# Last output tile written instead of accumulated, and list scatters without a memset behind their pacing copy

## The chip, the cores and the metric

The kernel runs on one core of a Trainium2 chip. The metric is the device time of one execution in microseconds (us). TensorE (PE) does the matmuls, VectorE (DVE) and ScalarE (ACT) empty the accumulators, GpSimd (POOL) issues the indirect DMAs and does some elementwise work, SyncE (SP) issues the plain DMAs.

## The reference

A linear attention with decay (4 batches, 8 heads, 768 positions, blocks of 64) gives 3072 tokens of 512 numbers. Behind it stands a mixture of 8 experts: each token goes to the two experts with the highest noisy logits, with two softmax weights, and its output row is the sum of the two experts' rows. Cut to what matters here:

```python
noisy_logits = x @ w_gate + log1p(exp(x @ w_noise)) * noise
top2 = argpartition(-noisy_logits, 2, axis=1)[:, :2]      # top2_w: softmax of the two
out = zeros((3072, 512))
for e in range(8):
    for k in range(2):
        mask = top2[:, k] == e
        h = maximum(x[mask] @ w1[e], 0.0)
        out[mask] += top2_w[mask, k, None] * (h @ w2[e])
```

Everything is float32; the kernel splits each factor of a matmul into a high and a low part and sums three products.

## The kernel before

The attention runs first, over twelve units of two chunks. While it runs, the routing works out, for each token and each of its two choices, a row of a list in DRAM (`lst`, one stretch per expert). 48 indirect DMAs on POOL (`scatter_list`, line 631) write 128 list entries each. They are not issued in one go: `routing` puts them into `scatters`, and `paced(n, tile)` (line 680) issues up to n of them at a chosen place of the program. `paced` first copies one element of a tile into a 1x1 `spacer` on POOL, so that POOL waits there until that tile has been made, and then calls `scatter(n)`, which calls `scatter_list` for each. `scatter_list` begins with a memset of the same `spacer` (line 633), then the indirect DMA (line 634). Some scatters are issued without `paced`, by `scatter` alone (from `finish` and in the main line).

Expert 0 is worked on with indices found directly. From expert 1 on an expert's list is read from DRAM (`load_rec`), its token rows are gathered (`gather_rows`, line 889, indirect DMAs on POOL), turned, split and multiplied by w1 (experts 2 to 7 by a scheme with seven products, `first_layer`), and then by w2 in tiles of 128 tokens (`gemm2`, line 1067). The experts 1 to 7 are ordered by load. Expert 7 of that order has six tiles, worked on in the order 0, 3, 1, 4, 2, 5; a list's unused places hold an index that is out of bounds, and the DMA skips it.

A tile of `gemm2` ends so: VectorE multiplies the accumulated rows by the tokens' weights (`tensor_scalar`, line 1094) into a staging tile, and `scatter_out` (line 1133) does a memset of `spacer` on POOL and an indirect DMA that writes the 128 rows to `out` (line 1135). For expert 0 it writes plainly; for the others it carries `compute_op` ADD, so that the DMA adds to what `out` holds. The scatters of one expert don't wait for one another; the first tile of an expert waits for those of the expert before. `out` is filled with zeros during the attention.

After the first layer of expert 7 POOL gets a `drain` (line 1474). Behind the last tile stands a loop for tokens beyond an expert's capacity (`For_i`, line 1520), with no iteration for these inputs. The tile `zero` (128 rows of 512) is used as a staging buffer when rows are turned, last for expert 7.

Of the kernel before, what the change touches and what calls it, by code (L numbers as in the profile page):

```python
# [37 lines left out]
E = 8  # L38
F = 1024
FB = F // 128  # L40
NTOK = B * S
# [44 lines left out]
def tiles(e):  # L86

    return NT if TAILS[e] else NT - 1


def size(e, t):
    return TS if t < NT - 1 else TAILS[e]
# [31 lines left out]
def kernel(  # L124
# [3 lines left out]
    nc = tc.nc  # L128
    MULT, ADD, SUB = OP.mult, OP.add, OP.subtract
# [62 lines left out]
    for i in range(7):  # L192
        n = 1 << i
# [3 lines left out]
    p = psum.tile([128, H], FT, name="pL")  # L197
# [13 lines left out]
    p = psum.tile([128, HP, C], FT, name="pL")  # L211
# [69 lines left out]
    jobs, scatters, PL = [], [], {}  # L281
# [15 lines left out]
        if all_scattered:  # L297
            scatter(len(scatters))

    def scatter(n):  # L300
        for job in scatters[:n]:
            scatter_list(*job)
        del scatters[:n]

    qT, qTs, kT, KD, AT, XO, XP, PO, SA, first = {}, {}, {}, {}, {}, {}, {}, {}, {}, {}
# [322 lines left out]
    lst_st, lst_ld = [], []  # L628
    spacer = consts.tile([1, 1], FT, name="spacer")

    def scatter_list(b, c, i):
        r = RT[b]
        nc.gpsimd.memset(spacer, 0.0)
        st = nc.gpsimd.indirect_dma_start(  # L634
            out=lst, out_offset=bass.IndirectOffsetOnAxis(ap=r["dest"][:, i, c:c + 1], axis=0),
            in_=r["rec"][:, c, i, :], in_offset=None)
        for s in lst_st:
            tc.declare_no_dep(st.ins, s.ins, reason="every pair of token and choice has its own row")
        for g, s in lst_ld:
            if g < b:  # L640
                tc.declare_no_dep(st.ins, s.ins, reason="a later group writes no row of an earlier group's part")
        lst_st.append(st)
# [37 lines left out]
    def paced(n, tile):  # L680
        if scatters:
            nc.gpsimd.tensor_copy(spacer, tile[0:1, 0:1])
            scatter(n)


    WB = wp.tile([128, (2 * DB - 1) * F], FR, name="w1")
# [6 lines left out]
    for n in range(2):  # L693
        o, m = n * DB * CAP, DB * TX * TS
# [11 lines left out]
    WS, REC, PV, HT, XB, WX = {}, {}, [], [], [], []  # L706
# [141 lines left out]
    def parts(e):  # L848
        if not e:
            return [(sum(PARTS0[:i]), n) for i, n in enumerate(PARTS0)]  # L850
        return [(0, PARTS1[0]), (PARTS1[0], PARTS1[1])]

    def tile_order(e):

        if e < 2:
            return [t0 + t for t0, n in parts(e) for t in range(n)]
        return [0, 3, 1, 4, 2, 5, 6][:tiles(e)]
# [198 lines left out]

    ahead = []
    OT = []

    def ring():  # L1060
        OT.append(OT.pop(0))
        return OT[-1]

# [3 lines left out]
    def gemm2(e, t):  # L1067
        n = size(e, t)
        p = psum.tile([128, DM], FT, name=next(bank2))
        if n == TS:  # L1070
            for i, (f, a, b) in enumerate(TERMS):
                if e < 2:
                    h = ht(e, a, f, slice(t * TS, t * TS + n))
                else:
                    h = hv(e, a, f, t // 3)[:, t % 3 * TS:(t % 3 + 1) * TS]
                if i == KEPT:
                    yield
                nc.tensor.matmul(p, h, W2[b][f // 2][:, f % 2, :], start=(i == 0), stop=(i == len(TERMS) - 1))  # L1078
        else:
            yield  # L1080
            for i in range(2 * FB):
                f, b = i // 2, i % 2
                nc.tensor.matmul(p[:2 * n, :], HT[0].rearrange("p (f c) -> p f c", f=FB)[:, f, FULL:FULL + 2 * n],
                                 W2[b][f // 2][:, f % 2, :], start=(i == 0), stop=(i == 2 * FB - 1))
        o = ahead.pop() if ahead else ring() if e else PV[t]
        w = REC[e, t][:, 1:2].bitcast(FT)
        if n < TS:
            o = o[:n, :]
            nc.scalar.activation(o, p[n:2 * n, :], AF.Copy)
            nc.vector.tensor_add(o, o, p[:n, :])  # L1090
            p = o
        if e in CROSS and n == TS:
            o, p = o.rearrange("p (b d c) -> p b d c", b=DB, c=32), p.rearrange("p (d b c) -> p b d c", b=DB, c=32)
        nc.vector.tensor_scalar(o, p, w, None, op0=MULT)  # L1094
        if e:
            scatter_out(e, t, o if n < TS or e not in CROSS else o.rearrange("p b d c -> p (b d c)"))

# [35 lines left out]
    def scatter_out(e, t, o):  # L1133
        nc.gpsimd.memset(spacer, 0.0)
        st = nc.gpsimd.indirect_dma_start(  # L1135
            out=out, out_offset=bass.IndirectOffsetOnAxis(ap=REC[e, t][:, 0:1], axis=0), in_=o, in_offset=None,
            bounds_check=NTOK - 1, oob_is_err=False, **({"compute_op": ADD} if e else {}))
        if t == 0:
            out_st.clear()
        for s in out_st:  # L1140
            tc.declare_no_dep(st.ins, s.ins, reason="an expert has a token once")
        out_st.append(st)

    zero = consts.tile([128, DM], FT, name="zero")
# [10 lines left out]
    for t in range(NST):  # L1155
# [19 lines left out]
        if u == NST:  # L1175
            scatter(1)
# [47 lines left out]
    XR.append(hp.tile([128, DM], FT, name="xr2"))  # L1224
    OT.extend(hp.tile([128, DM], FT, name=f"ot{i}") for i in range(5))
    PV.append(ring())
# [220 lines left out]
    for e in range(1, E):  # L1447
        if e == E - 1:
            n_over = nc.values_load(ntot[0:1, 0:1], min_val=0, max_val=MAXOV)
        if e == 1:  # L1450
            prepare(2)
            for i, (t0, n) in enumerate(parts(e)):
                for f in range(FB):
                    gemm1(e, t0, n, f)
                    if f >= 4:
                        next(ovj, None)
                    if i and f >= LAG:
                        turn_next(f - LAG)
                    if i == 0 and f % 2 == 0:
                        split_w(2, e, f // 2)  # L1460
                    if i and f < 2:
                        load_c(2, f)
                    if f < tiles(e):
                        nc.gpsimd.tensor_copy(spacer, ht(e, 0, f, columns(e, t0, n))[0:1, 0:1].bitcast(FT))
                        if t0 == 0:
                            scatter_out(0, f, PV[f][:size(0, f), :])
                        else:
                            gather_rows(2, tile_order(2)[f])
        else:
            if e == 2:  # L1470
                OT.insert(0, GT)
            step, todo = first_layer(e)
        if e == E - 1:
            nc.gpsimd.drain()
        if e == 1:
            WX.append(wp.tile([128, F], FT, name="w1b"))
            XB.append(hp.tile([128, 6 * 2 * HW], FR, name="xb"))
        if e in CROSS:
            cr = [ring() if j < NT - 1 else hp.tile([128, 128], FT, name="crt")
                  for j in CT]  # L1480
            steps = [columns2(e, d, cr) for d in range(DB)] + [gemm2(e, t) for t in (0, 1, 3, 4)]
        else:
            steps = [gemm2(e, t) for t in (tile_order(e) if e > 1 else range(NT))]
        if e > 1:
            next(steps[0])
            for i, (f, m) in enumerate(ENDS):
                step(len(SEQ) + i, f, m)
            for s in sorted(todo):
                for op in todo[s]:
                    op()  # L1490
            next(steps[1])
        if e + 1 < E:
            fetch_pairs(e + 1)
            if e > 1:
                fetch_rest(e + 1)
        if e + 2 < E and e not in CROSS:
            prepare(e + 2)
        for t, tile in enumerate(steps):
            if e == 1:
                turn_next(t + FB - LAG)  # L1500
            if e in CROSS and t == DB:
                ahead.append(ring())
                cx = [fetch_crossed(e, j) for j in CT]
                load_c(e + 1, 2)
                prepare(e + 2)
            behind(e, t)
            if e in CROSS and t > DB:
                for i in {DB + 1: (0, 1), DB + 2: (2,)}.get(t, ()):
                    add_crossed(e, CT[i], cx[i])
            last(tile)  # L1510
            if e in CROSS:
                if t == DB - 1:
                    for i, c in enumerate(cr):
                        nc.sync.dma_start(crossed[i], c)
            if e == 1:
                next(ovj, None)
                if t == 1:
                    fetch_rest(2)
    W1[1][DB - 1] = wp.tile([128, F], FR, name="w1b")
    with tc.For_i(0, n_over) as it:  # L1520
# [9 lines left out]
                                     bounds_check=NTOK - 1, oob_is_err=False)  # L1530
# [6 lines left out]
        for f in range(FB):  # L1537
            p = psum.tile([128, OV], FT, name="pS", bufs=4)
# [7 lines left out]
        p = psum.tile([OV, DM], FT, name="pO")  # L1546
        for f in range(FB):
            for i, (a, b) in enumerate(((0, 0), (0, 1), (1, 0))):
                nc.tensor.matmul(p, ht(0, a, f, slice(0, OV)), W2[b][f // 2][:, f % 2, :],
                                 start=(f == 0 and i == 0), stop=(f == FB - 1 and i == 2))  # L1550
        o = ring()[:OV]
        nc.vector.scalar_tensor_tensor(o, p, r[:, 1:2].bitcast(FT), zero, op0=MULT, op1=ADD)
        nc.gpsimd.indirect_dma_start(out=out, out_offset=off, in_=o, in_offset=None,
                                     bounds_check=NTOK - 1, oob_is_err=False)
# [27 lines left out]
```

## Time and profile before

| | us |
|---|---|
| median of 3 runs | 696.99 (695.52 to 699.48) |
| profiled execution | 693.23 |
| span of the profiled execution | 691.4 |

| engine | busy us | share of the span |
|---|---|---|
| PE | 671.6 | 97% |
| DVE | 482.4 | 70% |
| POOL | 370.0 | 54% |
| ACT | 309.5 | 45% |

The span runs from the first to the last recorded event of the profiled execution. "Idle before" is the time in which an engine had nothing running ahead of an instruction, with what ended it. Times "to landing" run from the start of a DMA's issuing instruction to the end of the transfer. A DMA issued by POOL has a row of its own on POOL (DMA_INDIRECT).

### The profile page before, as it was taken

The page shows a single profiled execution, that of the slowest core. Times are in us where ns is not written, and L with a number is a line of the kernel's source. Part 1 is how long each engine was busy: PE and PEld are TensorE (multiplying, and loading weights), DVE is VectorE, ACT ScalarE, POOL GpSimd, SP SyncE. Part 2 cuts the span into 40 slices and gives each one's busy share as a digit, 9 for nine tenths or more (in the row PEclk, how much of TensorE's full clock was granted, in tenths as well). Part 3 has the DMA queues.
Part 4 walks back from the last instruction along what each step waited for, and adds up shares of the span by engine and source line. Part 5 has one row for each costly group of instructions (what it writes and reads, how often), then busy time and mean ns, then how long its engine had stood idle before and what let it go on. Part 6 is the DMA issues. An engine that isn't in the chain of part 4 may idle for free.

```text
span 691.4 us, 13961 instructions
## 1 busy us (share of the span) xinstructions
PE 671.6 (97%) x4861; PEld 598.1 (87%) x4861; DVE 482.4 (70%) x1060; ACT 309.5 (45%) x634; POOL 370.0 (54%) x474
## 2 busy tenths in 40 slices
PE   7899999899999999999999999999999999999995
PEld 4788888698898898899989998998898899889984
DVE  6335888878436566789867886889596979588610
ACT  2667786441133332365437434653363356327400
POOL 7111355678854555776358536753773667264332
PEclk9999999999999999999999999999999999999998
DMA  9999999576517437766477547854875576464033
GB/s 205 214 233 262 229 252 250 163 245 163 113 32 221 136 119 171 175 177 191 149 183 188 189 149 178 221 175 142 166 235 158 126 195 189 122 135 116 1 46 40
DMA packets 151901, 115.06 MB, mean 166 GB/s; under 512 B 88063, under 2 KB 123007, under 8 KB 151828
## 3 DMA queue, kind: packets, MB, share of 16 engines
q1 hardware_dynamic: 137636, 84.04, 44.8%
q0 software_dynamic: 13776, 29.57, 20.5%
q8 instruction: 39, 0.64, 0.4%
q10 hardware_dynamic: 416, 0.53, 0.3%
q14 instruction: 34, 0.28, 0.1%
HBM read 77.58 MB, written 37.32 MB: 166 GB/s over the span
## 4 chain that ended last, share of the span: by engine, by line
PE 68%; DVE 12%; issue 8%; POOL 4%; DMA 3%; SPq 2%; ACT 1%; POOLq 1%; DVEq 0%
PE pS L993 15%; PE pKV L1078 13%; PE pO L1078 10%; PE pS L1037 7%; PE pS L1110 5%; PE pS L364 3%; PE pKV L377 2%; POOL lst L634 2%; PE pO L377 2%; SPq L160 2%; PE pR L993 1%; POOL out_dram L1135 1%; DMA xr<-x_tok,rec 1%; DVE ht L1004 1%; PE pS L437 1%
## 5 line engine op out<-in xcount | busy, mean ns | idle before, releaser
L993 PE MATMUL pS<-xa,w 128*128 128x400 f32 (+1 forms) x624 | 158.0, 343 | 0.3 <-ACT gt L1012 0.2
L818 POOL TENSOR_TENSOR wst<-wst 128x256 f32<-128x256 f32 x96 | 96.4, 1016 | 84.1 <-DVE w L810 81.7
L993 PEld LDWEIGHTS pS<-xa,w 128*128 128x128 f32 x624 | 113.2, 188 | 4.6 <-DVE w L810 2.0
L1135 POOL DMA_INDIRECT out_dram<-ot,rec x40 | 73.6, 1839 | 75.5 <-DVE ot L1094 56.2
L1078 PE MATMUL pKV<-w2h,ht 128*128 128x512 f32 x336 | 109.0, 394 | 0.0
L1078 PE MATMUL pO<-w2h,ht 128*128 128x512 f32 x336 | 108.4, 392 | 0.0
L993 PE MATMUL pS<-xb,w 128*128 128x400 f32 (+1 forms) x240 | 81.6, 340 | 0.0
L1078 PEld LDWEIGHTS pKV<-w2h,ht 128*128 128x128 f32 x336 | 63.2, 188 | 14.3 <-DVE gt L1094 0.6
L1078 PEld LDWEIGHTS pO<-w2h,ht 128*128 128x128 f32 x336 | 63.1, 188 | 13.5
L1037 PE MATMUL pS<-xa,w 128*128 128x256 f32 (+2 forms) x440 | 73.5, 316 | 0.8 <-DVE xa L901 0.4
L1037 PEld LDWEIGHTS pS<-xa,w 128*128 128x128 f32 x440 | 65.3, 189 | 4.9 <-DVE xa L901 0.6
L1078 PE MATMUL pKV<-w2l,ht 128*128 128x512 f32 x168 | 65.8, 391 | 0.0
L1078 PE MATMUL pO<-w2l,ht 128*128 128x512 f32 x168 | 65.7, 391 | 0.0
L961 ACT ACTIVATE xa<-wst 128x512 fp32r<-128x512 f32 (+1 forms) x48 | 25.1, 568 | 79.5 <-DVE wst L970 72.3
L810 DVE TENSOR_TENSOR w<-wst,w 128x512 fp32r<-128x512 f32 (+2 forms) x72 | 59.6, 844 | 0.1
L889 POOL DMA_INDIRECT xr<-x_tok,rec x42 | 46.2, 1101 | 19.2 <-issue 6.5
L634 POOL DMA_INDIRECT lst<-recs,dest x48 | 49.7, 1035 | 10.8 <-issue 8.5
L1012 ACT ACTIVATE ot<-pS 128x400 f32<-128x400 f32 (+1 forms) x60 | 29.7, 495 | 48.8 <-PE pS L993 44.6
L808 ACT ACTIVATE w<-wst 128x512 fp32r<-128x512 f32 (+2 forms) x72 | 48.1, 692 | 5.3 <-POOL wst L818 5.2
L1004 DVE SCALAR_TENSOR_TENSOR ht<-ot,ht 128x400 fp32r<-128x400 f32 (+1 forms) x60 | 45.4, 756 | 1.5 <-ACT ht L1001 0.8
L993 PEld LDWEIGHTS pS<-xb,w 128*128 128x128 f32 x240 | 45.0, 188 | 0.6 <-DVE xb L962 0.3
L1043 ACT ACTIVATE ht<-pS 128x256 fp32r<-128x256 f32 (+2 forms) x40 | 17.9, 448 | 59.5 <-PE pS L1037 58.2
(287 smaller groups left out, 1367.0 us busy)
## 6 DMA issues: line engine op xcount, KB each, us to landing
wst<-in_moe_w_dram SPq DMA_DIRECT2D x36, 512.0 KB, 5.4
wst<-in_moe_w_dram SPq DMA_DIRECT2D x32, 256.0 KB, 3.3
kt<-in_k_dram SPq DMA_DIRECT2D x24, 256.0 KB, 5.6
qt<-in_q_dram SPq DMA_DIRECT2D x24, 256.0 KB, 6.7
vt<-in_v_dram SPq DMA_DIRECT2D x24, 256.0 KB, 5.3
wst<-in_moe_w_dram SPq DMA_DIRECT2D x48, 128.0 KB, 3.4
wst<-turned SPq DMA_DIRECT2D x96, 64.0 KB, 2.0
turned<-w1b SPq DMA_DIRECT2D x20, 256.0 KB, 2.8
```

The costliest lines, as they stand in the source:

```text
L634: st = nc.gpsimd.indirect_dma_start(out=lst, out_offset=bass.IndirectOffsetOnAxis(ap=r["dest"][:, i, c:c + 1], axis=0), in_=r["rec"][:, c, ...
L808: nc.scalar.activation(hi[:, ks], src, AF.Copy)
L810: nc.vector.tensor_tensor(lo[:, ks], src, hi[:, ks].bitcast(FT), op=SUB)
L818: g.tensor_tensor(o, x, y, op=op)
L889: nc.gpsimd.indirect_dma_start(out=xrow(e, t)[:size(e, t)], out_offset=None, in_=x_tok[:rows, :], in_offset=bass.IndirectOffsetOnAxis(ap=a ...
L993: nc.tensor.matmul(p, WO[f % 2][:, a, kw, d, :], xo(x, kx, kx + 1)[:, 0, d, :w], start=first and i == 0, stop=i == 5, skip_group_check=True)
L1004: return lambda: nc.vector.scalar_tensor_tensor(hv(e, 1, i, k), src, 0.0, hv(e, 0, i, k).bitcast(FT), op0=OP.max, op1=SUB)
L1012: nc.scalar.activation(banks[m], U, AF.Copy)
L1037: nc.tensor.matmul(p, W1[a][d][:, fs], xt(b, cs)[:, d], start=(d == 0 and i == 0), stop=(d == DB - 1 and i == 2))
L1078: nc.tensor.matmul(p, h, W2[b][f // 2][:, f % 2, :], start=(i == 0), stop=(i == len(TERMS) - 1))
L1110: nc.tensor.matmul(p, W2[b][f // 2][:, f % 2, d * 128:(d + 1) * 128], h, start=(i == 0), stop=(i == len(TERMS) - 1))
L1135: st = nc.gpsimd.indirect_dma_start(out=out, out_offset=bass.IndirectOffsetOnAxis(ap=REC[e, t][:, 0:1], axis=0), in_=o, in_offset=None, bo ...
```

## The change

It has two parts. The last tile of expert 7 (`LAST`, expert 7, tile 5) no longer adds in the DMA: behind the drain an indirect DMA gathers the rows of `out` that this tile's tokens have so far into `zero`; the tile's last VectorE instruction becomes a `scalar_tensor_tensor` (accumulator times weight plus `zero`); and the scatter writes plainly. And the first list scatter behind each pacing copy loses its memset.

```diff
-    def scatter(n):
-        for job in scatters[:n]:
-            scatter_list(*job)
+    def scatter(n, spaced=True):
+        for j, job in enumerate(scatters[:n]):
+            scatter_list(*job, spaced or j > 0)
...
-    def scatter_list(b, c, i):
+    def scatter_list(b, c, i, spaced):
         r = RT[b]
-        nc.gpsimd.memset(spacer, 0.0)
+        if spaced:
+            nc.gpsimd.memset(spacer, 0.0)
...
     def paced(n, tile):
         if scatters:
             nc.gpsimd.tensor_copy(spacer, tile[0:1, 0:1])
-            scatter(n)
+            scatter(n, False)
...
+    LAST = E - 1, tile_order(E - 1)[-1]
...
-        nc.vector.tensor_scalar(o, p, w, None, op0=MULT)
+        if (e, t) == LAST:
+            nc.vector.scalar_tensor_tensor(o, p, w, zero, op0=MULT, op1=ADD)
+        else:
+            nc.vector.tensor_scalar(o, p, w, None, op0=MULT)
...
-            bounds_check=NTOK - 1, oob_is_err=False, **({"compute_op": ADD} if e else {}))
+            bounds_check=NTOK - 1, oob_is_err=False, **({"compute_op": ADD} if e and (e, t) != LAST else {}))
...
         if e == E - 1:
             nc.gpsimd.drain()
+            nc.gpsimd.indirect_dma_start(
+                out=zero, out_offset=None, in_=out,
+                in_offset=bass.IndirectOffsetOnAxis(ap=REC[LAST][:, 0:1], axis=0),
+                bounds_check=NTOK - 1, oob_is_err=False)
```

## Rows read from the trace of the kernel before

**Rows 1.** Busy time by stage: window, then per engine busy us (instructions), PEclk, DMA.
```profile
110.00:140.00 30.00, 25.98 (x394) 21.58 (x392) 25.62 (x94) 16.69 (x35) 17.62 (x35) 1.00 0.66 201
172.90:200.00 27.10, 27.10 (x171) 24.82 (x169) 10.05 (x37) 5.11 (x13) 22.00 (x52) 1.00 0.46 92
200.00:211.10 11.10, 11.09 (x64) 9.80 (x62) 2.63 (x9) 3.55 (x6) 4.68 (x5) 1.00 0.23 53
211.10:223.00 11.90, 11.84 (x64) 9.91 (x64) 8.64 (x12) 5.29 (x9) 4.46 (x6) 1.00 0.74 234
653.00:685.00 32.00, 30.54 (x136) 25.01 (x134) 6.62 (x10) 1.43 (x3) 8.48 (x12) 1.00 0.30 40
```

**Rows 2.** Timeline of VectorE and POOL at the end: start, duration, what [idle before].
```profile
683.58 0.75 DVE L1094 TENSOR_SCALAR ot<-pKV,rec 128x512 f32<-128x512 f32 x1 [4.74 <-PE pKV L1078]
684.61 1.56 POOL L1135 DMA_INDIRECT out_dram<-ot,rec  x1 [3.90 <-DVEq L1520]
```

**Rows 3.** DMA issues, windows from 684, 244, 241.5, 230 and 227: last, us to landing.
```profile
out_dram<-ot,rec POOLq DMA_INDIRECT x1, 4.5
...
out_dram<-zero,recz POOLq DMA_INDIRECT x1, 4.7
...
out_dram<-xb,recz POOLq DMA_INDIRECT x1, 2.7
...
out_dram<-xb,recz POOLq DMA_INDIRECT x1, 3.6
...
out_dram<-ot,recz POOLq DMA_INDIRECT x1, 4.9
```

**Rows 4.** DMA queue of POOL, windows 684.5:691.4 and 679:684.5: packets, MB, share.
```profile
q0 software_dynamic: 144, 0.19, 22.1%
...
q0 software_dynamic: 144, 0.26, 36.8%
```

**Rows 5.** Timeline of POOL: the four plain scatters of expert 0 with the landings above.
```profile
228.03 1.88 POOL L1135 DMA_INDIRECT out_dram<-ot,recz  x1 [0.78 <-issue]
...
230.94 1.00 POOL L1135 DMA_INDIRECT out_dram<-xb,recz  x1 [0.69 <-issue]
...
241.78 0.98 POOL L1135 DMA_INDIRECT out_dram<-xb,recz  x1 [0.72 <-DVE tail L749]
...
244.31 1.82 POOL L1135 DMA_INDIRECT out_dram<-zero,recz  x1 [0.74 <-DVE tail L753]
```

**Rows 6.** Timeline of VectorE, 226 to 230.
```profile
226.82 0.69 DVE L1047 SCALAR_TENSOR_TENSOR ht<-pS,ht 128x512 fp32r<-128x512 f32 x1 [1.72 <-ACT ht L1043]
227.77 1.23 DVE L846 TENSOR_TENSOR w2l<-wst,w2h 128x1024 fp32r<-128x1024 f32 x1 [0.26 <-ACT w2h L842]
```

**Rows 7.** Timeline of POOL behind the drain.
```profile
653.06 0.09 POOL L1134 MEMSET spacer<- 1x1 f32 x1 [5.48 <-issue]
661.26 1.56 POOL L1135 DMA_INDIRECT out_dram<-ot,rec  x1 [8.11 <-DVE ot L1094]
```

**Rows 8.** All gathers of line 889: duration ns min/median/max, then landing.
```profile
L889 POOL DMA_INDIRECT xr<-x_tok,rec x42: 925/1046/1493, 206.3 to 579.8; - x42
...
DMA to landing us min/median/max: 3.3/4.4/7.1
```

**Rows 9.** Timeline of POOL: a pacing copy, its memset, its list scatter; the last of them.
```profile
176.03 0.18 POOL L682 COPY spacer<-ht 1x1 f32<-1x1 f32 x1
176.26 0.09 POOL L633 MEMSET spacer<- 1x1 f32 x1
176.51 0.98 POOL L634 DMA_INDIRECT lst<-recs,dest  x1 [0.16 <-issue]
...
199.81 0.98 POOL L634 DMA_INDIRECT lst<-recs,dest  x1 [0.16 <-issue]
206.29 1.05 POOL L889 DMA_INDIRECT xr<-x_tok,rec  x1 [5.50 <-DMA rec<-lst]
```

**Rows 10.** Timeline of POOL: gathers behind a copy, with no memset between.
```profile
250.12 1.05 POOL L889 DMA_INDIRECT xr<-x_tok,rec  x1 [0.47 <-issue]
...
259.90 0.97 POOL L889 DMA_INDIRECT xr<-x_tok,rec  x1 [0.24 <-DVE ot L915]
```

**Rows 11.** The chain that ended last, 199.7 to 213: start, us, what.
```profile
199.81 4.08 DMA lst<-recs,dest
...
207.65 3.47 DMA xr<-x_tok,rec
211.12 0.04 issue
211.16 0.66 PE pS L898 x4
```

## The prediction, made before the change was run

> **What bounds the kernel now.** I read the busy times first, then the windows by stage, then the chain of waits, and then the timeline at the two places that the change touches. TensorE is busy for 671.6 of the span's 691.4 us, so an edit off TensorE counts only where TensorE stands still. The windows show three such places: the load at the start, some 4 us between 110 and 140 us, where VectorE is the busy one (25.62 of 30 us, POOL 17.62), and the end. From 172.9 to 211.1 us TensorE is busy for 38.19 of 38.2 us, and in the last 32 us before 685 for 30.54 [rows 1].
>
> The end is a chain with nothing beside it: VectorE's last instruction (683.58 to 684.33), 0.28 us to POOL, the indirect scatter from 684.61, landed 4.5 us later at about 689.1, and 2.3 us of closing until the span ends at 691.4 [rows 2, 3]. What shortens this chain shortens the kernel one for one.
>
> The list scatters are the second place. The chain of waits runs along POOL from 175 to 200 us, over the last list scatter (landed 4.08 us after 199.81), the reading of the list and the gather of its rows, to TensorE at 211.16 [rows 9, 11]. It looks like a bound, but TensorE is full up to that point: the two chains arrive together, and I count 0.07 us of stall there at most (11.84 of 11.90 us and 11.09 of 11.10 busy around it [rows 1]).
>
> **The last scatter without ADD.** Its issue takes 1.56 us [rows 2]. The plain scatters of expert 0, from the same line and with the same bounds check, take 0.98 to 1.00 us where VectorE leaves POOL alone, and 1.82 to 1.88 where it doesn't: at 228.03 a 1.23 us VectorE subtraction from 227.77 lies over the issue [rows 5, 6]. At 684 VectorE has finished for good, so I take 0.98.
>
> The Trainium skill says why such a row differs ("SBUF — State Buffer", section "SBUF: two separate sides"): some VectorE instructions take a port pair away from GpSimd for their whole length, and GpSimd can't write DMA descriptors meanwhile. The trace agrees: 229.00, where that subtraction ends, plus 0.90 is the scatter's end at 229.91.
>
> Its landing, counted from the start of the issue, was 4.5 us. Plain ones landed after 2.7 us (241.78), 3.6 (230.94), 4.7 (244.31) and 4.9 (228.03) [rows 3, 5]; the last two are those with the long issue. The nearest is the 2.7: an issue of 0.98 us, and queues otherwise near empty. So the gain is 4.5 - 2.7 = 1.8 us, with the ends 4.5 - 4.9 = -0.4 and, since the last tile moves only 0.19 MB where a full one moves 0.26 [rows 4], a little more than 1.8: at most a quarter of the 1 us or so that a full plain transfer can have of these 2.7, so 2.1.
>
> **VectorE's last instruction.** A scalar_tensor_tensor of 128x512 from the accumulator with a second input took 0.69 us [rows 6], the tensor_scalar 0.75 [rows 2]: -0.06 us, on the path.
>
> **The added gather.** One indirect DMA on POOL behind the drain, where POOL then waits until 661.26 for its first output scatter [rows 7]. Gathers cost POOL 0.93 to 1.49 us and land 3.3 to 7.1 us after the issue begins [rows 8]. From 653.06 plus some 0.3 us it lands between 656.7 and 660.5. It reads what the experts before have added, and their last scatter was issued at about 622, so it doesn't wait for that. Behind it on POOL stand the memset and the first scatter of expert 7, which must now wait for the gather, since it writes `out` too. That scatter waits for VectorE until about 661.0 anyhow, so the new wait costs nothing. With the cover gone, a late gather would first push scatters that have 3.4 to 3.9 us of idle before each of them; the last VectorE instruction needs the gathered rows only at 683.6. Its data, 0.19 MB at most, falls into a stretch with a DMA share of 0.30 [rows 1]. Zero, then; at worst a few hundredths for one more semaphore at the end.
>
> **The missing memsets.** 32 of the 48 list scatters stand directly behind a pacing copy and lose theirs. From the end of the copy (176.21) to the DMA (176.51) pass 0.30 us, of which the memset has 0.09 [rows 9]. Without it the trace has gathers behind a copy: 0.24 us where the cleanest stands, 0.47 at another [rows 10]; the least is the 0.16 that follows the memset now. So the edit is worth between -0.14 and +0.17 us per scatter, and I take the cleanest row, -0.06. POOL works without a pause from 149 us on; 21 of the 32 lie there, 13 of them after 172.9. Taken together the last list scatter comes some 1.3 us earlier. That meets a TensorE that is full [rows 1]: worth at most the 0.07 us of stall. The eleven before 149 us lie where VectorE sets the pace, so nothing either.
>
> **The sum.** 1.8 + 0.06 + at most 0.07: about 1.9 us, of which I take 1.8, leaving a tenth for the added semaphore. The profiled execution would come from 693.23 (span 691.4 and 1.83 around it) to 691.4. It lies 3.8 us below the median of the runs, 696.99; the chain at the end has the same length in both, so the median comes to 695.2.
>
> **Rivals.**
> - The landing is fixed behind the issue. The two plain scatters with long issues landed 3.02 (4.9 - 1.88) and 2.88 us (4.7 - 1.82) after it, the ADD one 2.94 (4.5 - 1.56): as though plain and ADD finished alike [rows 2, 3, 5]. Then only the issue is saved, 0.58, plus 0.06: 0.6 us, 696.4. Against it: 2.7 - 0.98 = 1.72 us at 241.78. The Trainium skill speaks for this rival ("DMA: Bandwidth & Descriptors", section "Anatomy of one DMA — SWDGE (gpsimd) path"): a fixed 2 us or so, mostly the receipt of the write, plus bytes over bandwidth, with no term for an add.
> - The memset hid the start of the scatter, and without it the gap grows (slower than before). If the 0.47 us between a copy and a gather is what a scatter behind a copy needs, each paced list scatter costs 0.17 us more. POOL has no pause from 149 us on, so 21 of them add up to 3.6 us at 199.81, and since TensorE meets the gathered rows with no slack at 211.16, it stands still for 3.5 of them [rows 9 to 11]. Net of the 1.8: +1.7, 698.7. It decides from 0.09 us per scatter on (21 times that is 1.9). Against it: the gathers carry a bounds check that the list scatters don't, and one of them needs only 0.24.
> - Earlier lists are worth something after all, if TensorE's idle 4 us before 140 hang on POOL in some way: 11 x 0.14 = 1.5 us more, 693.7. Against it: VectorE is the busy engine there.
> - The gain isn't there: DMA landing as at 228.03, -0.4 + 0.06, 697.3.
>
> **How the numbers follow.** Likeliest (gain of 1.3 to 2.1 us) 0.57, fixed landing 0.18, slower gap 0.08, earlier lists 0.10, no gain 0.07. A measurement of this kernel can tell about 0.5%, 3.5 us, from no change; only the spread of the runs (695.52 to 699.48) carries any case beyond that. Faster by more than that: 0.12, out of the likeliest and the earlier lists with a lucky median; slower: 0.05, from the growing gap; the rest, 0.83, within. The range goes from the earlier lists less 1 us of spread, 692.7, to somewhat under the growing gap, 698.2.
>
> **What would show it.** In the changed profile: the last DMA_INDIRECT of line 1135's scatter at 0.98 us (right) or 1.5 (wrong); its landing at 2.7 (right) or 3.9 (the fixed-landing rival); the end of the span 2.3 us behind it; the added gather started near 653.4 and landed before 661, with the first scatter of expert 7 still waiting for VectorE. The gap between pacing copy and list scatter, 0.24 expected, decides the second part, with the last list scatter near 198.5 and TensorE still above 38.1 of 38.2 us between 172.9 and 211.1. A gap above 0.39, or TensorE waiting at the transposes near 211 us, makes the second rival right and the prediction wrong.

## The result

The changed kernel is slower: 704.0 us (median of 22 runs, 698.27 to 708.24) against 699.68 for the kernel before beside it (22 runs, 695.52 to 704.05), a ratio of 1.0063 with a 95% interval of 1.0044 to 1.0082. Its profiled execution took 704.2 us, span 702.3, against 693.23 and 691.4 before.

The end did what was forecast in kind. Timeline of the changed kernel, the added gather and the last tile; columns as in [rows 2]:

```profile
666.39 1.08 POOL L1480 DMA_INDIRECT zero<-out_dram,rec  x1 [6.54 <-issue]
...
673.53 1.58 POOL L1140 DMA_INDIRECT out_dram<-ot,rec  x1 [5.97 <-DVE ot L1099]
...
695.85 0.75 DVE L1097 SCALAR_TENSOR_TENSOR ot<-pKV,rec,zero 128x512 f32<-128x512 f32 x1 [4.74 <-PE pKV L1080]
...
696.88 1.05 POOL L1140 DMA_INDIRECT out_dram<-ot,rec  x1 [3.90 <-DVEq L1529]
```

The gather starts behind the drain, and the first scatter of expert 7 still waits for VectorE, 5.97 us. The last scatter's issue takes 1.05 us where [rows 2] have 1.56, and from its start to the end of the span pass 702.3 - 696.88 = 5.42 us, before 691.4 - 684.61 = 6.79. So 1.37 us are won there, and the loss is elsewhere. Windows of the changed kernel (the last is the stretch that [rows 1] have from 172.9 us), then the three of the kernel before that answer to its middle ones; columns as in [rows 1]:

```profile
110.00:140.00 30.00, 25.51 (x386) 20.90 (x385) 25.57 (x95) 15.52 (x34) 15.15 (x25) 1.00 0.63 178
140.00:166.00 26.00, 23.72 (x196) 21.74 (x195) 17.74 (x79) 7.95 (x18) 20.76 (x33) 1.00 0.82 253
166.00:200.00 34.00, 29.16 (x184) 25.97 (x183) 15.44 (x58) 4.11 (x11) 18.80 (x31) 0.85 0.32 75
200.00:212.00 12.00, 12.00 (x76) 11.42 (x76) 4.59 (x12) 3.05 (x7) 8.30 (x15) 1.00 0.13 25
212.00:223.00 11.00, 11.00 (x64) 9.92 (x63) 2.32 (x9) 3.64 (x6) 4.05 (x5) 1.00 0.21 52
...
172.90:200.00 27.10, 24.93 (x166) 23.11 (x167) 12.24 (x50) 3.03 (x9) 15.89 (x26) 0.82 0.40 93
```

```profile
140.00:166.00 26.00, 25.74 (x199) 23.41 (x200) 21.29 (x89) 7.74 (x17) 20.41 (x37) 1.00 0.81 233
166.00:200.00 34.00, 34.00 (x244) 31.64 (x242) 14.78 (x58) 6.28 (x16) 27.55 (x59) 1.00 0.41 83
200.00:212.00 12.00, 11.93 (x70) 10.60 (x69) 3.53 (x10) 4.29 (x8) 5.28 (x6) 1.00 0.26 67
```

TensorE, full before, is idle here. Over 110 to 223 us its busy time falls from 108.65 us (25.98 of [rows 1], 25.74, 34.00, 11.93, and 11.00 in the last eleven) to 101.39: 7.3 us. And from 172.40 to 182.64 us its granted clock is 0.50, the lower of its two levels (1.2 and 2.4 GHz). TensorE is busy for 7.69 of these 10.24 us and does about half of the work in them, so some 3.8 us more are lost. Together 11.1 us; the span grew by 10.9, and with the 1.37 won at the end 12.3 have to be found. The account closes but for 1.2 us.

Timeline of the changed kernel at that place, in the order of engines PE, DVE, ACT, POOL:

```profile
162.91 0.34 PE L549 MATMUL pL<-ob,ones 128*128 128x8 bf16 x8
163.59 0.60 PE L899 MATMUL pS<-identf,xb 128*128 128x128 f32 x4
...
172.14 0.38 PE L1038 MATMUL pS<-xa,w 128*128 128x256 f32 x1 [1.95 <-ACT xa L901]
175.07 2.50 PE L1038 MATMUL pS<-xa,w 128*128 128x256 f32 x10 [2.55 <-DVE xa L902]
...
178.66 2.71 PE L1038 MATMUL pS<-xa,w 128*128 128x256 f32 x11
...
183.37 1.48 PE L1038 MATMUL pS<-xa,w 128*128 128x256 f32 x11
...
169.59 0.17 DVE L560 SCALAR_TENSOR_TENSOR own<-ob,pL 128x8 f32<-128x8 bf16 x1 [6.27 <-remote]
...
171.00 1.08 ACT L901 ACTIVATE xa<-pS 128x512 fp32r<-128x512 f32 x2 [14.83 <-PE pKV L1080]
...
156.63 0.99 POOL L635 DMA_INDIRECT lst<-recs,dest  x1 [0.15 <-issue]
...
157.96 0.99 POOL L635 DMA_INDIRECT lst<-recs,dest  x1 [0.15 <-issue]
...
168.37 0.97 POOL L635 DMA_INDIRECT lst<-recs,dest  x1 [0.22 <-issue]
179.41 1.04 POOL L890 DMA_INDIRECT xb<-x_tok,idx  x1 [10.07 <-DVE found L605]
...
211.44 0.99 POOL L635 DMA_INDIRECT lst<-recs,dest  x1 [0.16 <-issue]
```

VectorE's line 560 needs the matmuls of line 549, whose records end at 163.25. It starts at 169.59, 6.3 us later, and ScalarE's line 901, which needs the turned rows of line 899 (to 164.19), at 171.00. What these two make is then late for TensorE, which waits at 172.14 and again at 175.07. In this stretch its clock falls: eleven matmuls take 2.71 us at 178.66, and 1.48 at 183.37, when the clock is full again. POOL's gathers wait 10.07 us for the late indices, and the last of the list scatters behind them starts at 211.44 instead of 199.81 [rows 9]. In the kernel before the matmuls of line 549 ended at 159.72, and VectorE started line 560 at once; two scatters of its run of list scatters stand below:

```profile
159.38 0.34 PE L549 MATMUL pL<-ob,ones 128*128 128x8 bf16 x8
...
159.76 0.17 DVE L560 SCALAR_TENSOR_TENSOR own<-ob,pL 128x8 f32<-128x8 bf16 x1
...
155.59 0.99 POOL L634 DMA_INDIRECT lst<-recs,dest  x1 [0.16 <-issue]
...
157.07 0.98 POOL L634 DMA_INDIRECT lst<-recs,dest  x1 [0.16 <-issue]
```

That lag, from the end of line 549's matmuls to VectorE's line 560, is the quantity to follow: 0.04 us before, 6.3 after. It is TensorE's side of it that is late. The trace also has the time of each update of a semaphore, the signal that a waiting engine looks for. The update by line 549's matmuls stands at 169.56 us, 0.03 before line 560 starts; those by line 899's matmuls stand at 170.98 and 171.04, and ScalarE's line 901 starts at 171.00. So VectorE and ScalarE start at once when the update comes. In the kernel before it stands at 159.74, 0.02 behind the end of the matmuls.

### The profile page after: what moved, and what is told of

Its sections match the earlier page's. It is cut to its first block, busy times and chain, and to the rows that moved or that the text cites. A ratio compares the mean times of both kernels' runs of the same rounds, so it can differ in the third digit from the quotient of the medians.

```text
span 702.3 us, 13931 instructions
## 1 busy us (share of the span) xinstructions
PE 676.4 (96%) x4861; PEld 601.5 (86%) x4861; DVE 483.0 (69%) x1060; ACT 309.3 (44%) x634; POOL 367.5 (52%) x443
## 5 line engine op out<-in xcount | busy, mean ns | idle before, releaser
L994 PEld LDWEIGHTS pS<-xa,w 128*128 128x128 f32 x624 | 113.1, 188 | 4.7 <-DVE w L811 2.1
L1038 PE MATMUL pS<-xa,w 128*128 128x256 f32 (+2 forms) x440 | 76.6, 325 | 5.3 <-DVE xa L902 3.0
L1038 PEld LDWEIGHTS pS<-xa,w 128*128 128x128 f32 x440 | 67.9, 197 | 9.9 <-DVE xa L902 3.4
```

The lines of the kernel that those rows point to most:

```text
L994: nc.tensor.matmul(p, WO[f % 2][:, a, kw, d, :], xo(x, kx, kx + 1)[:, 0, d, :w], start=first and i == 0, stop=i == 5, skip_group_check=True)
L1038: nc.tensor.matmul(p, W1[a][d][:, fs], xt(b, cs)[:, d], start=(d == 0 and i == 0), stop=(d == DB - 1 and i == 2))
```

## The experiments

They were run in five sessions. In the first and the fourth the kernel before took 695.3 and 695.7 us in the median, in the second, third and fifth 701.3, 700.5 and 700.8 (beside the result above, 699.7). The first two were on one chip (number 12), the others on three more (7, 14 and 2); so the same chip gave both levels, and what differs between the sessions is not known. I call them the 695 and the 700 sessions, because the whole finding turns on them. Ratios are to the kernel before of the same session. The theories' names are those of each expectation.

### Session 1 (before: 695.3 us): each part alone

The last tile alone, with its gather behind the drain; list scatters as before:

```diff
+        if (e, t) == LAST:
+            nc.vector.scalar_tensor_tensor(o, p, w, zero, op0=MULT, op1=ADD)
...
+            bounds_check=NTOK - 1, oob_is_err=False, **({"compute_op": ADD} if e and (e, t) != LAST else {}))
```

> Only the last tile's part of the change; every list scatter keeps its memset. Theory A (the loss lies in the list scatters, between 100 and 220 us; the tail is a small gain): 1.4 us under the kernel before, as the changed profile's end is shorter (696.88 to 702.3 is 5.4 us, where before it was 684.61 to 691.4, 6.8). Theory B (the loss comes from the added gather and the new order at the end): 4 to 6 us over the kernel before. Theory C (both kernels stall now and then in that stretch, and the two profiles were drawn at opposite ends): within 1.5 us of the kernel before.

Measured: 693.7 us, ratio 0.9971 [0.9949, 0.9993]: 1.6 us under the kernel before, as theory A asked. Its last scatter and its DMAs (to landing) at the end:

```profile
684.47 1.05 POOL L1140 DMA_INDIRECT out_dram<-ot,rec  x1 [3.90 <-DVEq L1529]
```

```profile
out_dram<-ot,rec POOLq DMA_INDIRECT x1, 3.3
...
zero<-out_dram,rec POOLq DMA_INDIRECT x1, 3.3
```

The plain scatter landed after 3.3 us, the one with ADD after 4.5 [rows 3]; from issue to the end of the span pass 690.2 - 684.47 = 5.73 us instead of 6.79.

The missing memsets alone:

```diff
-        nc.gpsimd.memset(spacer, 0.0)
+        if spaced:
+            nc.gpsimd.memset(spacer, 0.0)
...
-            scatter(n)
+            scatter(n, False)
```

> Only the missing memsets; the last tile is as in the kernel before. Theory A: 5 to 7 us over the kernel before, with TensorE standing still between 160 and 200 us and its clock down for some 10 us. Theory B: as the kernel before, within 1 us. Theory C: within 1.5 us of the kernel before, and its profile may show a stall or not.

Measured: 692.99 us, 0.9976 [0.9956, 0.9995]: here this part wins, 2.3 us in the medians, which none of the three theories allowed. Its timeline of POOL and its windows:

```profile
156.52 0.18 POOL L683 COPY spacer<-ht 1x1 f32<-1x1 f32 x1
156.86 0.98 POOL L635 DMA_INDIRECT lst<-recs,dest  x1 [0.16 <-issue]
...
198.92 0.98 POOL L635 DMA_INDIRECT lst<-recs,dest  x1 [0.16 <-issue]
```

```profile
172.90:200.00 27.10, 27.10 (x170) 24.82 (x169) 9.49 (x34) 5.09 (x12) 21.12 (x37) 1.00 0.39 88
200.00:211.10 11.10, 11.10 (x66) 9.95 (x65) 3.00 (x10) 3.55 (x6) 4.21 (x5) 1.00 0.26 66
```

The gap between copy and scatter is 0.16 us (156.70 to 156.86), the last list scatter starts 0.9 us earlier than in [rows 9], and TensorE is full, as forecast.

The memset in front of the pacing copy instead of behind it (the rest of this edit is as in the list part), and two memsets ahead of every list scatter:

```diff
     def paced(n, tile):
         if scatters:
+            nc.gpsimd.memset(spacer, 0.0)
             nc.gpsimd.tensor_copy(spacer, tile[0:1, 0:1])
-            scatter(n)
+            scatter(n, False)
```

> The kernel before, with the memset put in front of the pacing copy in place of behind it: as many instructions on POOL, but the list scatter stands directly behind the copy. If the loss is that the scatter follows the copy directly: 5 us over the kernel before, as with no memset. If it is that POOL's list scatters come too close together in time (a memset less, 0.13 us less between them): within 1 us of the kernel before, since the spacing stays where POOL works without a pause.

```diff
         nc.gpsimd.memset(spacer, 0.0)
+        nc.gpsimd.memset(spacer, 0.0)
         st = nc.gpsimd.indirect_dma_start(
```

> The kernel before with two memsets in front of every list scatter. If the spacing of the list scatters decides, in the direction that less costs, more of it costs nothing or gains 0 to 3 us against the kernel before; by the prediction's view (the lists' chain meets a full TensorE at 211 us with no slack) each memset more costs up to 0.1 us for some 48 scatters, 2 to 4 us over the kernel before.

Measured: 694.27 us, 0.9987 [0.9964, 1.0009], and 701.52 us, 1.0097 [1.0062, 1.0133]. The first decides nothing, since the list part itself doesn't lose in session 1. The second loses 6.2 us, more than the 2 to 4 that were expected at most. TensorE's waits of the second between 200 and 223 us (total, times, longest), and its POOL:

```profile
PE pS L899 <- DMA xr<-x_tok,rec: 7.2, 2, 5.1
```

```profile
205.18 0.98 POOL L635 DMA_INDIRECT lst<-recs,dest  x1 [0.16 <-issue]
212.16 1.05 POOL L890 DMA_INDIRECT xr<-x_tok,rec  x1 [6.00 <-DMA rec<-lst]
```

With the last list scatter 5.4 us later than in [rows 9], TensorE stands for 7.2 us at the gathered rows: the place without slack that the second rival named is real. But the changed kernel shortens that chain, so this is not its loss.

### Session 2 (before: 701.3 us): both parts

The changed kernel again, and the changed kernel with a memset in front of each pacing copy:

```diff
         if scatters:
+            nc.gpsimd.memset(spacer, 0.0)
             nc.gpsimd.tensor_copy(spacer, tile[0:1, 0:1])
             scatter(n, False)
```

> The changed kernel itself, on a chip beside fresh runs of the kernel before, since each part alone came out faster (0.9971 and 0.9976 of the kernel before) and the whole slower (1.0063). Theory A' (the two parts add up; what made the whole slower is a disturbance that came with the chip or the session of that comparison): 0.995 of the kernel before, some 3.5 us faster, and no stall of VectorE and ScalarE between 160 and 200 us in its profile. Theory B' (the two parts together do what neither does alone): 1.005 or more, with that stall, on this chip too.

> The changed kernel with a memset again for each pacing copy, in front of the copy. Theory A': 0.996 of the kernel before, about as the last tile's part alone. Theory B': if the missing POOL instructions are what the last tile's part meets, no loss here (0.996) while the changed kernel itself loses; if it is the scatter directly behind the copy, 1.005 here as well.

Measured: 707.02 us, 1.0094 [1.0058, 1.0130], and 699.86 us, 0.9986 [0.9954, 1.0018]. Line 549 and line 560 of the first:

```profile
163.89 0.34 PE L549 MATMUL pL<-ob,ones 128*128 128x8 bf16 x8
...
170.26 0.17 DVE L560 SCALAR_TENSOR_TENSOR own<-ob,pL 128x8 f32<-128x8 bf16 x1 [5.97 <-remote]
```

The loss and the lag come back (line 560 6.0 us behind the matmuls), and a memset per paced scatter, put where it no longer stands between copy and scatter, takes the loss away. So it is not that gap that costs; the loss goes with the number of POOL's instructions, and so with how densely POOL issues. In the changed kernel's run of list scatters one issue follows another after 1.33 us (156.63 to 157.96), before after 1.48 (155.59 to 157.07).

### Session 3 (before: 700.5 us): the parts beside one another

> The missing memsets alone, beside both parts together on the same chip in the same stretch of time. Theory A'' (the missing memsets alone lose, but only where VectorE and ScalarE wake late from TensorE's semaphore, as in the profile of the changed kernel; the tail part gains about 0.3% everywhere): where the kernel before has its longer time (about 700 us), the ratio is 1.008 to 1.013, with TensorE busy for 34 us or less of 166 to 200; where it has its shorter time (about 695 us), 0.9976 as already seen. Theory B'' (the loss needs both parts in one program): 0.995 to 1.000 here whatever the kernel before does, and a loss only in the run with both parts. Theory C'' (the loss is not from the edits but from the executions: some of them have late semaphores, whatever the kernel): the time of this kernel falls into two groups like those of the others.

> The last tile alone, beside the others. Theory A'': 0.997 +- 0.002 on any chip, no stall between 110 and 212 us beyond that of the kernel before, and if this chip is the slower one its trace lacks some semaphore records as that of the changed kernel does. Theory B'': the same time. Theory C'': as the others, two groups. If the tail part alone loses, both A'' and B'' fall.

> Both parts, beside each part alone. Theory A'': the product of the two ratios next to it; 1.005 to 1.010 where the kernel before takes about 700 us, 0.994 to 0.997 where it takes about 695. Theory B'': 1.005 to 1.010 on either, above each of the parts alone. Theory C'': two groups of times, as the parts.

> Both parts with a memset put in front of each pacing copy, so that POOL issues as many instructions as before in another order. Theory A'': between the kernel before and the changed one, 0.997 to 1.001 where the kernel before takes about 700 us, 0.996 where it takes about 695. Theory B'': 0.997 to 1.000. Theory C'': as the others.

Measured, in this order: 704.71 us, 1.0073 [1.0043, 1.0102]; 697.56 us, 0.9971 [0.9945, 0.9997]; 702.78 us, 1.0046 [1.0018, 1.0074]; 698.71 us, 0.9976 [0.9950, 1.0002]. The product of the first two is 1.0044: the parts add, and theory B'' falls. The list part alone makes the loss here, while it won in session 1; the last tile wins the same 0.3% in both. That is theory A'' in the main: it asked for 1.008 to 1.013 from the list part, and for no stall in the tail alone, whose TensorE is busy for 2.1 us less between 110 and 212 us than the kernel before's (95.53 and 97.65). Theory C'' doesn't hold for the times: the kernel before's 35 runs spread from 695.71 to 703.73 without two groups, and those of the list part lie higher, from 699.88 to 707.25. Timelines of the list part and of the last tile alone at line 549 and line 560:

```profile
162.96 0.34 PE L549 MATMUL pL<-ob,ones 128*128 128x8 bf16 x8
...
170.01 0.17 DVE L560 SCALAR_TENSOR_TENSOR own<-ob,pL 128x8 f32<-128x8 bf16 x1 [6.65 <-remote]
...
170.75 1.09 ACT L901 ACTIVATE xa<-pS 128x512 fp32r<-128x512 f32 x2 [14.83 <-remote]
```

```profile
160.97 0.34 PE L549 MATMUL pL<-ob,ones 128*128 128x8 bf16 x8
...
162.25 0.17 DVE L560 SCALAR_TENSOR_TENSOR own<-ob,pL 128x8 f32<-128x8 bf16 x1 [0.88 <-PE pS L899]
```

### Sessions 4 and 5: where in the list part it lies

Between 149 and 169 us POOL of the kernel before issues 13 list scatters with hardly a pause, eight of them behind a pacing copy. Three kernels are to tell whether it is this run; `PACED` counts the calls of `paced` (the lines that do so are not shown). The eight alone left out:

```diff
-            scatter(n)
+            scatter(n, not 12 <= len(PACED) <= 19)
```

All but the eight left out:

```diff
-            scatter(n)
+            scatter(n, 12 <= len(PACED) <= 19)
```

All left out, with one pause ahead of the copy at 160 us:

```diff
+            if len(PACED) == 17:
+                for _ in range(12):
+                    nc.gpsimd.memset(spacer, 0.0)
             nc.gpsimd.tensor_copy(spacer, tile[0:1, 0:1])
-            scatter(n)
+            scatter(n, False)
```

The fourth has the last tile's part together with the second of these forms. Session 4 (before: 695.7 us):

> Only the eight memsets behind the pacing copies between 150 and 170 us are left out; the other 24 stand. Theory D1 (the run of list scatters from 150 to 169 us, without the 0.13 us per issue, holds up the wake-ups of the other engines until it ends): most of the loss of the list part, 1.004 to 1.007, if the kernel before takes about 700 us here, with VectorE's instruction that waits for the matmuls of the positions (line 560) idle for 4 us or more before it. Theory D2 (the loss is made by the 13 after 172 us, whose lists come earlier and collide there): 0.998 to 1.001, no such wait. Theory D3 (every missing memset costs its share, wherever it stands): a quarter, about 1.002. Where the kernel before takes about 695 us all of them expect 0.998 to 1.000.

> The reverse: the eight memsets between 150 and 170 us stand, the other 24 are left out. Theory D1: 0.998 to 1.002 if the kernel before takes about 700 us, VectorE at line 560 idle for under 2.5 us. Theory D2: 1.005 to 1.008. Theory D3: three quarters, about 1.0055.

> All 32 memsets left out as in the list part alone, and twelve memsets in a row in front of the one pacing copy at 160 us, some 1.6 to 2.8 us in which POOL issues no DMA. Theory D1: the wake-ups come in the pause, VectorE at line 560 is not held up by 6 us, and the ratio falls from 1.0073 to 1.000 to 1.003 if the kernel before takes about 700 us. Theories D2 and D3: 1.006 to 1.008, as without the pause, since the list chain is no slower than the kernel before's. A theory that POOL's instructions as such hold up the others, not its DMAs: no better than without the pause, or worse.

> The last tile's part, and the memsets left out but for the eight between 150 and 170 us. Theory D1: 0.995 to 0.999, level with the last tile alone (0.997), better than both parts together (1.005). Theory D2: 1.002 to 1.005. Theory D3: 1.0025.

Measured: 693.11 us, 0.9973 [0.9958, 0.9988]; 692.79 us, 0.9965 [0.9952, 0.9979]; 693.01 us, 0.9970 [0.9957, 0.9982]; 690.47 us, 0.9936 [0.9920, 0.9952]. All win about what the list part won in session 1, the last with the 0.3% of the tail on top. For the first that is more than the 0.998 to 1.000 that all theories asked for at this level, for the last more than any range; nothing is told apart here. The same again in session 5 (before: 700.8 us), with the changed kernel beside them:

> As before, only the eight memsets between 150 and 170 us left out. Where the kernel before takes about 700 us: theory D1 (the run of list scatters holds up the wake-ups) 1.004 to 1.007 with over 4 us of idle before VectorE's line 560; D2 (the 13 later ones) 0.998 to 1.001; D3 (each its share) 1.002. Where it takes about 695: 0.997 again.

> All 32 memsets left out, the run broken at 160 us. Where the kernel before takes about 700 us: D1 1.000 to 1.003, the idle time before line 560 gone; D2 and D3 1.006 to 1.008. Where it takes about 695: 0.997 again.

> The last tile's part, and 24 memsets left out, the eight between 150 and 170 us kept. Where the kernel before takes about 700 us: D1 0.995 to 0.999; D2 1.002 to 1.005; D3 1.0025. Where it takes about 695: 0.994 again.

> The changed kernel. Where the kernel before takes about 700 us: 1.005 to 1.009 again, by all theories. Where it takes about 695, the product of the parts that were timed there, 0.9971 times 0.9976: 0.9947, so 0.993 to 0.997, the change as it was forecast; a loss there would mean that the two parts together lose whatever the kernel before takes.

Measured: 704.52 us, 1.0050 [1.0024, 1.0075]; 702.2 us, 1.0023 [1.0004, 1.0043]; 701.7 us, 1.0003 [0.9978, 1.0029]; 704.64 us, 1.0047 [1.0021, 1.0073]. Timelines of the first (the eight alone), of the second (the pause) and of the third (the eight kept, with two of its list scatters) at the same two lines:

```profile
164.53 0.34 PE L549 MATMUL pL<-ob,ones 128*128 128x8 bf16 x8
...
169.98 0.17 DVE L560 SCALAR_TENSOR_TENSOR own<-ob,pL 128x8 f32<-128x8 bf16 x1 [5.05 <-remote]
```

```profile
161.89 1.70 POOL L688 MEMSET spacer<- 1x1 f32 x12
...
163.89 0.34 PE L549 MATMUL pL<-ob,ones 128*128 128x8 bf16 x8
...
164.27 0.17 DVE L560 SCALAR_TENSOR_TENSOR own<-ob,pL 128x8 f32<-128x8 bf16 x1
```

```profile
155.38 0.98 POOL L635 DMA_INDIRECT lst<-recs,dest  x1 [0.16 <-issue]
...
156.85 1.03 POOL L635 DMA_INDIRECT lst<-recs,dest  x1 [0.16 <-issue]
...
162.29 0.34 PE L549 MATMUL pL<-ob,ones 128*128 128x8 bf16 x8
...
168.69 0.17 DVE L560 SCALAR_TENSOR_TENSOR own<-ob,pL 128x8 f32<-128x8 bf16 x1 [2.94 <-remote]
```

A quarter of the missing memsets makes most of the loss (0.50% of the list part's 0.73%, which was measured in another session and with an interval that overlaps), and the other 24 some 0.3% (1.0003 over the tail's 0.9971). Per memset that is 0.06% against 0.013%, so D3 is too even (its 1.002 for the eight alone lies just under the interval, its 1.006 for the pause well above), and D2 has the wrong place. D1 holds for two of its three kernels; for the third it asked for 0.999 at most and got 1.0003, with an interval that reaches to 0.9978. The trace of that third kernel speaks against D1: POOL issues one list scatter per 1.47 us (155.38 to 156.85), as in the kernel before, and the lag is 6.1 us all the same. With the pause the lag is gone (0.04 us), but the kernel still loses 0.2%, and its trace has an update of TensorE's semaphore 6.2 us late at 189 us instead. So by the times the run of issues is the main place, not the only one, and a dense run is not needed for the lag. The changed kernel came out a little under the 1.005 to 1.009 expected.

The lag against the time of each profiled execution, all eleven profiles taken where the kernel before took about 700 us. The last column is for that update of TensorE's semaphore, anywhere in the trace, that comes longest after the end of the last matmul before it that makes one (if it belongs to an earlier matmul, it is later still):

| profile | its own time, us | lag at line 560, us | longest delay of an update, us |
|---|---|---|---|
| both and swap, session 2 | 696.4 | 1.6 | 2.1 |
| both, session 3 | 697.0 | 1.0 | 4.4 |
| tail | 697.6 | 0.9 | 1.7 |
| both and swap, session 3 | 700.1 | 2.1 | 2.6 |
| list with pause | 701.7 | 0.04 | 6.2 |
| both, session 5 | 703.7 | 2.5 | 4.0 |
| both, the result | 704.2 | 6.3 | 5.4 |
| both, eight kept | 704.3 | 6.1 | 6.5 |
| list | 706.2 | 6.7 | 6.6 |
| the eight alone | 706.2 | 5.1 | 4.1 |
| both, session 2 | 707.2 | 6.0 | 5.4 |

The same kernel shows both: with both parts, 697.0 us with a lag of 1.0 and 707.2 with 6.0. The lines of the former:

```profile
162.65 0.34 PE L549 MATMUL pL<-ob,ones 128*128 128x8 bf16 x8
...
163.96 0.17 DVE L560 SCALAR_TENSOR_TENSOR own<-ob,pL 128x8 f32<-128x8 bf16 x1 [0.91 <-PE pS L899]
```

So the memsets don't make the lag or forbid it, and one profile of each kernel can't tell how often it comes. The last column divides them: 1.7 to 2.6 us in the three kernels with as many POOL instructions beside the list scatters as before, 4.0 to 6.6 in the eight with memsets missing. The number of updates that are over 0.3 us late doesn't divide them: it is 18 to 25 in each. All of these fall between the first list scatter and 4.1 us behind the last one (106.7 to 215.5 us in the result's profile), among 66 to 78 that are recorded there. Of the 364 to 374 outside none is late, though POOL goes on with some 100 indirect DMAs of token rows. In the profile of the kernel before and in the eight of the 695 sessions none is late anywhere. So what delays TensorE's updates goes with the list scatters and with the session, in every kernel; what goes with the missing memsets is how long the longest delay is. In the 695 sessions' profiles of the last tile, the list part and the pause the lag is 0.04 to 0.05 us.

## Why the prediction was wrong

Forecast were 695.2 us, and 698.2 at most; measured were 704.0, 4.3 over the kernel before.

**The step that failed** is the cost of the missing memsets: earlier list scatters meet a full TensorE, "worth at most the 0.07 us of stall", so nothing. It asked only what becomes of POOL's own chain and never what the denser issuing does to other engines. TensorE's cover was taken as given from 172.9 to 211.1 us; in the changed kernel the run of scatters just before that stretch goes with an update of TensorE's semaphore 6.3 us late, for which VectorE waits and then TensorE itself: it is busy for 24.93 of those 27.10 us from 172.9 on, at a granted clock of 0.82. The edit costs 0.73% alone (5.1 us of 700.5). That the missing POOL instructions are at work, and not what stands between copy and scatter, the swapped kernel shows (0.9986 and 0.9976 with the tail's 0.9971 in it); that the run from 150 to 169 us is the main place, the eight alone show by their time. That it works by the density of the issues is argued, not shown: the kernel with the eight kept has the old density there and the lag too. By what path the list scatters delay TensorE's updates is not shown.

**The step from the profile to the median** failed with it. The profiled execution lay 3.8 us under the median, and I carried the saving over because the last chain "has the same length in both". That offset may have been the sign that most executions weren't like the one I read: with 22 runs the kernel before stands at 699.68, not 696.99. In the 695 sessions, which are like the profile, the step on the memsets holds in its sign: TensorE full (38.20 of 38.20 us), the ratio not above 1. In size it doesn't: leaving out all, eight or 24 of the memsets wins 0.24 to 0.35% there, where 0.07 us was the most. The change as a whole was not timed there; the parts multiply to 0.9971 x 0.9976 = 0.9947.

**The last scatter** was right in direction and mis-sized. Forecast 1.8 us; issue to end of span went from 6.79 to 5.42 (changed kernel) and 5.73 (tail alone), so 1.1 to 1.4. The issue took 1.05 for 0.98, the landing 3.3 for 2.7. The fixed-landing rival asked for 2.94 us behind the issue; it was 3.3 - 1.05 = 2.25, so the ADD costs in the issue (0.51) and behind it (0.7). The Trainium skill ("DMA: Bandwidth & Descriptors", section "Anatomy of one DMA — SWDGE (gpsimd) path"), whose fixed cost has no term for an add, stood for that rival, and the trace speaks against it. In time the last tile is worth 0.29%, 2.0 us of 695 with an interval of 0.5 to 3.5: the forecast's 1.8 lies in it, and so does what the trace shows.

**VectorE's last instruction** took 0.75 us, not 0.69: nothing won. **The gather** cost nothing, as argued: 1.08 us of issue, landed after 3.3, and the scatter behind it waited for VectorE all the same.

**The gap** between copy and scatter fell to 0.16 us, below the 0.24 I took and at the lower end, 0.14 less; the last list scatter came 0.9 us earlier instead of 1.3.

**The rivals.** The second named the right sign, but a loss of 1.7 us where 4.3 were measured, and by a gap that grows; it shrank. Its second half, that a later list chain stops TensorE, is confirmed only by the kernel with two memsets. Earlier lists may be worth what the third rival said: the list part won 0.24% (1.7 us) in session 1, and the profiles don't show where (25.83 us of VectorE and 26.04 of TensorE between 110 and 140, before 25.62 and 25.98). Its fastest run is no faster than the kernel before's (692.22 and 692.0); what it lacks are the slow ones (693.83 at most, before 700.31).

**What stays open.** What makes a 695 or a 700 session. One thing goes with it: in the profiles of the 700 sessions the trace lacks some semaphore records (the changed kernel: 450 of TensorE's 472, 873 of VectorE's 961), in those of the 695 sessions next to none (all of TensorE's, at least 960 of VectorE's), with the same kernels. Whether that is a cause or another effect, no run here tells; nor whether the recording itself has a part in the late updates. Nor is it shown that the kernel before has such lags itself in a 700 session: its profile is of another kind. The tail alone, which issues its list scatters just as the kernel before does, has 18 late updates there, 1.7 us at most.

The kernel to keep is the last tile's part with the memsets left alone: 0.9971 in both kinds of session. With 24 memsets taken out as well it is the fastest seen, 690.47 us (0.9936), but only where the kernel before takes 695.7; where it takes 700.8 it gains nothing (1.0003).

## What to carry to other kernels

An instruction that looks like idle filler between DMA issues can matter to other engines: before it is taken out for a tenth of a microsecond, ask what the denser run may do to wake-ups elsewhere, and time the edit in more than one session. A profile that lies well under the median may be one of the lucky executions, and what hides an edit there need not hide it in the others. Parts of a change that touch different stages are worth timing apart: here one won 0.3% everywhere, and the other lost 0.7% or won 0.2%.

## What was not expected of the hardware

- In five profiles VectorE, waiting on TensorE, started 5 to 7 us after the matmuls' records ended (163.25 to 169.59 in the changed kernel), in a run in which POOL issued list scatters every 1.33 us (1.47 in one of the five); in the same stretch of a 695 session, at the same rate, it started after 0.04 us. The trace has the update of TensorE's semaphore itself late (169.56). In three of the five the wake-up came after the run's last issue had ended (0.25, 0.9 and 1.6 us), in the other two while POOL was still issuing.
- An indirect scatter with ADD cost more behind its issue as well, with one scatter of each kind at the same place: landing 4.5 us against 3.3, of which the issue is 1.56 against 1.05.
- Twelve memsets of one element on POOL took 1.70 us, 0.14 each, in a row.
